# A gated unit and a long convolution on one core: an eleventh product on all rows, kernel-generation products in one block, other TensorE costs in the planner

## The chip, the cores and the metric

The kernel runs on one core of a Trainium2 chip. The metric is device time in microseconds, as the median of several runs. TensorE (PE) multiplies matrices and writes to PSUM; VectorE (DVE), ScalarE (ACT) and GpSimd (POOL) work on elements; SyncE (SP) issues most of the transfers. Each engine works through its own list of instructions in order, and waits between engines go by semaphores.

## The reference

The input is one sequence of 2048 tokens with 448 channels. The output mixes two branches with a gate per token:

```python
g = sigmoid((x * gate_w).sum(-1, keepdims=True))
# a: a long convolution per channel, its kernel a sum over 256 complex modes
dt = exp(log_dt)
A = -exp(log_A_real) + 1j * A_imag
C = (C_real + 1j * C_imag) * dt[:, None]
P = exp((A * dt[:, None])[:, :, None] * arange(2048)[None, None, :])
K = 2.0 * einsum("dn,dnl->dl", C, P).real
a = causal_convolution(x, K) + x * D_skip          # by FFT of length 4096
# b: a gated linear unit with 1792 hidden units
b = (sigmoid(x @ w_gate) * (x @ w_up)) @ w_down
out = g * a + (1 - g) * b
```

All is float32.

## The kernel before

Three streams of work share the engines.

**The gated unit** goes through the tokens in two halves H of two blocks B of 512, and through the hidden units in 14 tiles f of 128. To keep float32 accuracy with TensorE's fast format, every operand is split into a high and a low part: `wh` and `wl` of the weights, high and low blocks of the tokens in `xs`. `glu_mm` makes one 128 x 512 result in PSUM (`gu`) out of 448 input channels in eleven products. For each of three blocks of 128 channels there are three: high by high (L995), high weights by low tokens (L996), low weights by high tokens (L997). The last 64 channels are held twice, on rows 0-63 and on rows 64-127: block 3 of `xs` has the high parts of the tokens on the lower rows and their low parts on the upper rows, and block 3 of the weights holds the same 64 channels on both. So one product over 128 rows (L999) gives two of the three terms. The eleventh (L1000) takes the low weights by the high tokens, and uses rows 0-63 alone. `glu_up` calls `glu_mm` twice, for the gate and for the value, and joins them with a tanh on ScalarE (L983) and two operations on VectorE (L984, L987); `glu_down` multiplies the result by `w_down` in products of 448 columns (L1012 to L1014), and VectorE adds them up in `ob` (L1028).

**Kernel generation** (`kgen`, 28 chunks of 16 channels, each in two halves of 128 modes) computes the convolution kernels K. In a half-chunk, TensorE makes phases from positions (L827, L842), ScalarE takes sines and cosines into `ec` and `fr` (L844, L859), VectorE makes powers of the decay in `es` (three times L866) from tables `tb` that GpSimd builds, and multiplies (L881 to L885): L884 ends `ec`, L885, the last, ends `es`. Then the contraction over the modes: 16 products of 128 rows by 32 columns from `ec` and 16 from `es` (L890), all added into the one PSUM tile `kp`. `ec` and `es` have two buffers each.

**The transforms** are class `Chain`: u's spectrum, then for each half of the channels the spectrum of K, its product with u's (L500 to L507), and the way back (L546). First stages work on 64 rows (L442, L433), the spectra (L471) and the last stage (L546) on 64 columns of TensorE's array; L511 works on all of it. Two transposes go through memory by DMA (`shf`), two are done by VectorE (L453).

The order of everything is worked out when the kernel is built, by class `Plan`. Each operation is recorded with its engine, an assumed cost in ns, what it reads and writes, and a priority. `Plan.order` then runs a list schedule: at each step it takes the engine that can start first, and on it the ready operation with the smallest priority number. It follows buffers as they become free, and adds 1300 ns where ScalarE has to change its function table. The outcome is a fixed order for every engine; in the run itself only the semaphores count. Generation has priority 20, the chains of K 40 and 41, and the gated unit's products 60, so that the gated unit fills the gaps of the others. The costs of TensorE work come from `c_mm`; a group of 16 products of the generation has `KPC`, 680 ns.

Of the kernel before, what the change touches and what calls it, by code (L numbers as in the profile page):

```python
# [19 lines left out]
NCH = 28            # chunks of 16 channels  # L20
HD = 224            # channels of one half
NF = 14             # tiles of 128 hidden units
# [3 lines left out]
SPC, KPC, ACC = 640.0, 680.0, 93.0  # L26
# [17 lines left out]
# channel order of the kernel generation: (half, chunk, column tile, q)  # L44
# [8 lines left out]
def shape_tables():  # L53
    """Transform matrices and position grids: functions of the shapes alone."""
    l1, k1 = np.arange(64)[:, None], np.arange(64)[None, :]
    s1 = np.zeros((64, 32, 128), np.float32)
    t1 = np.zeros((128, 32, 64), np.float32)
    row = np.empty(64, np.int64)
    for k in range(64):
        row[k] = (k // 32) * 64 + (k % 32)  # L60
    for l2 in range(32):
        ph = 2.0 * np.pi * (((4 * k1 + 1) * (32 * l1 + l2)) % 8192) / 8192.0
        s1[:, l2, row] = np.cos(ph)
        s1[:, l2, row + 32] = -np.sin(ph)
        t1[row, l2, :] = np.cos(ph).T / 2048.0
        t1[row + 32, l2, :] = -np.sin(ph).T / 2048.0
    a, b = np.arange(32)[:, None], np.arange(32)[None, :]
    w = 2.0 * np.pi * ((a * b) % 32) / 32.0
    cw, sw = np.cos(w), np.sin(w)
    m = np.zeros((128, 256), np.float32)  # L70
    for g in range(2):
        re, im = slice(64 * g, 64 * g + 32), slice(64 * g + 32, 64 * g + 64)
        # rows (g c l2) to the real parts (g k2), then to the imaginary ones
        kr, ki = slice(32 * g, 32 * g + 32), slice(64 + 32 * g, 64 + 32 * g + 32)
        m[re, kr], m[im, kr] = cw, sw
        m[re, ki], m[im, ki] = -sw, cw
        # rows (c g k2) to rows (g c l2), the inverse
        ir, ii = slice(128 + 64 * g, 128 + 64 * g + 32), slice(128 + 64 * g + 32, 128 + 64 * g + 64)
        m[kr, ir], m[ki, ir] = cw, -sw
        m[kr, ii], m[ki, ii] = sw, cw  # L80
    pos = np.zeros((96, 16, 2, 32), np.float32)
    for d in range(16):
        pos[d, d, 0] = np.arange(32)
        pos[16 + d, d, 0] = np.arange(32)
        pos[32 + d, d, 0] = -1.0
        pos[48 + d, d, 0] = -1.0
        pos[64 + d, d, 1] = np.arange(32) + 0.5
        pos[80 + d, d, 1] = np.arange(32) + 0.5
    s1 = s1.reshape(64, 32 * 128)
    s1h = ((s1.view(np.uint32) + np.uint32(0x800)) & np.uint32(0xFFFFF000)).view(np.float32)  # L90
    return (np.concatenate([s1, s1h, s1h, s1 - s1h]), np.ascontiguousarray(t1.reshape(128, 32 * 64)),
            m, pos.reshape(96, 1024), np.eye(128, dtype=np.float32))


# functions that one table set of ScalarE holds
# [3 lines left out]
class Res:  # L99
    """Something that instructions read and write: a virtual tile or a DRAM tensor."""  # L100
# [43 lines left out]
class Plan:  # L144
    """Records instructions with what they touch, orders them for all engines by a list
    schedule (a ready instruction of the least priority number first) and emits them."""
# [9 lines left out]
    def op(self, eng, cost, fn, r=(), w=(), prio=0, after=(), size=0, table=None):  # L156
        me = dict(i=len(self.ops), eng=eng, cost=cost, fn=fn, prio=prio, size=size, table=table,
# [27 lines left out]
    def order(self):  # L185
# [14 lines left out]
        wire, table, seq, left = 0.0, (), [], len(ops)  # L200
# [15 lines left out]
        while left:  # L216
# [19 lines left out]
            if o["table"] is not None and o["table"] not in table:  # L236
                table = next(x for x in TABLES if o["table"] in x)
                cost += 1300.0
            free[e] = te + cost
# [55 lines left out]
def c_mm(n, passes=1):  # L295
    return (max(0.4167 * n, 106.0) + 3.0) * passes


# priorities, least first
# [9 lines left out]
def gated_mix(ctx: ExitStack, tc, u, ut, aim, cre, cim, ldt, dskip, gw,  # L309
# [6 lines left out]
    def dma(dst, src, size, r, w, prio, **kw):  # L316
        """dst and src: functions that give the access patterns when emitted"""
        return op("SP", SPC, lambda: nc.sync.dma_start(dst(), src()), r=r, w=w, prio=prio, size=size, **kw)
# [10 lines left out]
    us = [dt_([128, 32, HD], f"us{h}") for h in halves]       # rows (s g k2) x (r c): columns k1 = 2 r + s  # L329
# [37 lines left out]
    def evac(dst, p, w, prio, n=D):  # L367
        """dst: function that gives the access pattern"""
        op("Act", c_act(n), lambda: S.activation(dst(), p[:, :n], AF.Copy), [p], w, prio)

    class Chain:
        """a half's channels in one tile [128, 32, HD], through the stages in place"""
# [13 lines left out]
        def move(self, pool, ps, bufs):  # L386
            """later stages: other buffers, and a second place for results"""
            self.pool, self.ps, self.bufs, self.suffix = pool, (self.ps[0], ps), bufs, "x"
# [7 lines left out]
        def stage1(self, src, ap):  # L396
            """[64 l1, 32 l2, channels] -> rows (g c k1)"""
# [23 lines left out]
        def stage1_split(self, th, tl, r, l):  # L421
            """rows 0-63: high parts of the input, rows 64-127: its low parts"""
# [11 lines left out]
            op("PE", c_mm(HD, 4), f, [th, tl, y], [p], prio)  # L434
            evac(lambda: self.pair(r), p, [*xr, (x, r)], prio)

        def stage1_pair(self, tb, r, l):
# [5 lines left out]
            op("PE", c_mm(HD, 8), f, [tb, (self.x, r)], [p], self.prio)  # L443
            evac(lambda: self.pair(r), p, [(self.x, r)], self.prio)

        def transpose(self):
            """rows (g c k) x columns l become rows (g c l) x columns k"""
# [16 lines left out]
        def spectrum_pair(self, r):  # L464
            """columns k1 = 2 r + s: real and imaginary parts of rows (s g k2)"""
            p = self.psum()

            def f():
# [4 lines left out]
            op("PE", c_mm(HD, 8) + 100, f,  # L473
               [(self.x, r), *([] if self.on_dve else [(self.x, ("t", i)) for i in range(4)]), m_sb], [p], self.prio)
# [14 lines left out]
        def product(self, us):  # L489
            """the kernels' spectrum times u's, and the first stage back"""  # L490
# [6 lines left out]
        def product_pair(self, ua, r):  # L497
            x, prio, ub = self.x, self.prio, self.tile("ub", (128, 2, 2, HD))
            p = self.spectrum_pair(r)
            op("DVE", c_dve(2 * D), lambda: V.tensor_mul(      # Ur Kr, Ur Ki, Ui Kr, Ui Ki  # L500
# [10 lines left out]
            op("PE", c_mm(D, 4), lambda: T.matmul(z[:, :D], m_sb[:, 128:256], self.pair(r), start=True, stop=True),  # L511
# [3 lines left out]
        def back(self, q):  # L515
            """tiles j in [4q, 4q + 4): the first half of the tokens is stored, the others' is added to the
            gated unit's part"""
# [21 lines left out]
        def back_j(self, j, tb, o, hs):  # L539
# [3 lines left out]
            def f():  # L543
# [4 lines left out]
            op("PE", c_mm(HD, 4) + 100, f,  # L548
               [tb, (x, j), *([] if self.on_dve else [(x, ("t", i)) for i in range(4)])], [p], self.prio)
# [13 lines left out]
    def gate(q, prio):  # L563
        """tiles 4q to 4q + 3"""
# [16 lines left out]
    def params(prio):  # L581
# [22 lines left out]
        class A:  # L604
            """a tile with a view"""
# [16 lines left out]
        # dt = exp(log_dt)  # L622
# [27 lines left out]
        def frac(dst, scr):  # L650
            """dst becomes round(dst) - dst"""
            act(scr, dst, AF.Copy, bias=MAGIC)
            stt(dst, scr, MAGIC, dst, ALU.subtract, ALU.subtract)
# [9 lines left out]
        # powers r^1, r^8, r^64, r^512 of r = exp(-exp(log_A_real) dt), modes on partitions: the  # L663
        # rational form in tanh, its quotient taken by one correction of the table's exponential
# [19 lines left out]
        def silu():  # L684
            """leaves the set with sine and hyperbolic tangent"""
# [4 lines left out]
        # phase of C in turns, and 2 |C| dt  # L690
# [16 lines left out]
        tt(rt, rt, mx, ALU.add)                      # |psi| in [0, 1/2]  # L707
        ts(mx, ci, 0.0, -2.0, ALU.is_lt, ALU.mult)
        stt(mx, mx, 1.0, rt, ALU.add, ALU.mult)      # psi
# [8 lines left out]
        # frequency in turns  # L718
        per_t(ai, ai, dtp)
        w, a64 = ci, acr  # L720
        frac(ai, w)                                  # -phi
        split(ai, 4)
        act(a64, ai, AF.Copy, scale=64.0)
        frac(a64, w)                                 # 64 phi
        split(a64, 0)
        stt(mx, ai, -31.5, mx, ALU.mult, ALU.add)
        frac(mx, w)                                  # -(psi + 31.5 phi)
# [55 lines left out]
    def powers(c, bs, prio):  # L783
        """for 16 channels: r^0..7, r^(8 0..7), r^(64 0..7), amplitude r^(512 0..3)"""
# [34 lines left out]
    def turns(c, nh, i, ph, fr, tp, ec, on_pe, prio):  # L819
        """the phase x in turns, less its nearest integer"""  # L820
# [27 lines left out]
    def half_chunk(c, nh, ph, tb, kp, prio):  # L848
# [37 lines left out]
        for e in (ec, es):  # L886
            def g(e=e):
# [5 lines left out]
            op("PE", KPC, g, [e], [kp], prio)  # L893

    def kgen(c, prio):
# [20 lines left out]
        if cc == 13:  # L916
            # u D is the convolution with D at the position 0: row 0 of every column tile
# [12 lines left out]
    def glu_xz(x, z, t0, prio):  # L930
        """blocks 0-2: high parts, 4-6: low parts; block 3: high on the rows 0-63, low on the others"""
# [41 lines left out]
    def glu_up(H, f, B, pe, prio):  # L973
# [8 lines left out]
        # 2 sigmoid(g) = 1 + tanh(g / 2); the half is in og  # L982
# [7 lines left out]
    def glu_mm(x, wh, wl, cs, pe):  # L990
        p = gps.tile("gu", GUB, (128, 512))

        def g(k):
# [4 lines left out]
            else:  # L998
                T.matmul(p.real, wh[:, 3, cs], x[:, 3], start=False, stop=False)  # L999
                T.matmul(p.real, wl[0:64, 3, cs], x[0:64, 3], start=False, stop=True)  # L1000
# [103 lines left out]
def host_arrays(inputs):  # L1104
# [8 lines left out]
    w1 = np.stack([blocks(g["B_w_gate"]), blocks(g["B_w_up"])], 3)      # k p f gu c  # L1113
# [26 lines left out]
```

## Time and profile before

| what | us |
|---|---|
| median of three runs | 883.9 |
| the three runs | 888.26, 883.9, 881.62 |
| span of the profiled execution, first to last instruction | 878.0 |
| first half-chunk of generation ends on VectorE | 162 |
| last half-chunk ends | 642 |

The profile is one execution. Its own whole time isn't recorded apart from its span, so the span is set against the median: 5.9 us lie outside it. A row of the timeline, of the waits or of the groups names an engine, a line of the kernel, and the tiles it writes and reads. Matmuls are pipelined: one that starts every 0.24 us can take 0.40 us from start to end, so that PE counts as busy through short pauses, and what a product costs is read from the distance of starts. A product in full float32 leaves two records, so that a group of 16 is 32 records.

### The profile page before, as it was taken

The numbers are of one execution on the slowest core, as the hardware profiler recorded it, in microseconds if no ns is written. First come the engines' busy times: TensorE is split into PE (matmuls) and PEld (weight loads), VectorE is DVE, ScalarE is ACT, GpSimd is POOL, SyncE is SP. The second block draws the span as 40 slices with busy tenths as digits, with TensorE's granted clock in tenths as the row PEclk, the third lists the DMA queues.
The fourth block names the chain that finished last, engine by engine and source line by source line (L and its number), as shares of the span: only waits on it lengthen the run. The fifth ranks groups of instructions, "written<-read, shape, count | busy, mean of one in ns | idle before, by whom it ended". The sixth has DMA issues, their size and how long they took to land. (4 is left out here: it accounts for less than half of the span.)

```text
span 878.0 us, 16776 instructions
## 1 busy us (share of the span) xinstructions
PE 808.5 (92%) x6688; PEld 541.5 (62%) x6688; DVE 733.0 (83%) x982; ACT 501.3 (57%) x862; POOL 330.1 (38%) x358
## 2 busy tenths in 40 slices
PE   4988799999988999999998999999989999889987
PEld 2665576666655667776665666666766566445543
DVE  2869984798995999999897989899846788978995
ACT  3544654677766877777677987777722352221210
POOL 3367644454452645374355535645021120000000
PEclk9989999899997999999999999999999999998999
DMA  9951377222290326436494116422959953294324
GB/s 242 226 107 32 97 216 168 95 95 93 81 194 26 125 83 146 160 116 157 135 219 120 44 60 180 125 84 79 208 104 248 280 153 109 70 212 119 85 56 117
DMA packets 95831, 115.66 MB, mean 132 GB/s; under 512 B 31465, under 2 KB 80937, under 8 KB 95241
## 3 DMA queue, kind: packets, MB, share of 16 engines
q1 hardware_dynamic: 93704, 110.98, 48.4%
q0 software_dynamic: 2048, 3.61, 1.6%
q8 instruction: 53, 0.87, 0.4%
q14 instruction: 26, 0.20, 0.1%
HBM read 78.32 MB, written 36.24 MB: 130 GB/s over the span
## 5 line engine op out<-in xcount | busy, mean ns | idle before, releaser
L995 PE MATMUL gu_gps<-xs_glu,wh_glu 128*128 128x512 f32 x336 | 148.0, 440 | 11.7 <-ACT wh_glu L969 11.6
L866 DVE TENSOR_TENSOR es_eg<-tb_eg 128x512 f32<-128x512 f32 x168 | 125.5, 772 | 20.7 <-PE kp_egp L890 19.2
L997 PE MATMUL gu_gps<-xs_glu,wl_glu 128*128 128x512 f32 x336 | 135.3, 403 | 1.2 <-POOL wl_glu L971 1.2
L996 PE MATMUL gu_gps<-xs_glu,wh_glu 128*128 128x512 f32 x336 | 135.5, 403 | 0.0
L1012 PE MATMUL dn_gps<-vh_glu,hh_glu 128*128 128x448 f32 x224 | 98.6, 440 | 7.0 <-ACT ob_glu L1021 3.5
L971 POOL TENSOR_TENSOR wl_glu<-xr_glu,wh_glu 128x512 fp32r<-128x512 f32 x44 | 77.8, 1777 | 65.7 <-ACT wh_glu L969 65.7
L995 PEld LDWEIGHTS gu_gps<-xs_glu,wh_glu 128*128 128x128 f32 x336 | 65.6, 195 | 41.2 <-issue 19.0
L1013 PE MATMUL dn_gps<-vh_glu,hl_glu 128*128 128x448 f32 x224 | 83.7, 374 | 4.5 <-DVE hl_glu L987 4.5
L1014 PE MATMUL dn_gps<-vl_glu,hh_glu 128*128 128x448 f32 x224 | 83.6, 373 | 0.5 <-POOL vl_glu L971 0.5
L884 DVE TENSOR_TENSOR ec_eg<-ec_eg,es_eg 128x1024 f32<-128x1024 f32 x56 | 79.8, 1426 | 0.0
L997 PEld LDWEIGHTS gu_gps<-xs_glu,wl_glu 128*128 128x128 f32 x336 | 65.3, 194 | 18.0 <-POOL wl_glu L971 2.8
L813 POOL TENSOR_TENSOR tb_eg<-tb_eg 128x96 f32<-128x96 f32 (+2 forms) x84 | 73.4, 877 | 5.8
L827 PE MATMUL tp_egp<-pos_sb,ph_eg 96*128 96x512 f32 x168 | 72.5, 446 | 1.9 <-ACT fr_eg L845 1.7
L885 DVE TENSOR_TENSOR es_eg<-fr_eg,es_eg 128x1024 f32<-128x1024 f32 x56 | 73.3, 1310 | 0.3
L996 PEld LDWEIGHTS gu_gps<-xs_glu,wh_glu 128*128 128x128 f32 x336 | 65.8, 196 | 10.0 <-issue 1.3
L971 POOL TENSOR_TENSOR vl_glu<-vr_glu,vh_glu 128x448 fp32r<-128x448 f32 x24 | 35.5, 1477 | 87.0 <-ACT vh_glu L969 85.5
L1012 PEld LDWEIGHTS dn_gps<-vh_glu,hh_glu 128*128 128x128 f32 x224 | 42.9, 191 | 39.0 <-issue 17.1
L803 POOL MEMSET tb_eg<- 128x96 f32 x28 | 7.8, 283 | 152.0 <-DVE es_eg L866 152.0
L1028 DVE SCALAR_TENSOR_TENSOR ob_glu<-dn_gps,og,ob_glu 128x448 f32<-128x448 f32 x72 | 49.1, 681 | 18.4 <-PE dn_gps L1014 17.7
L859 ACT ACTIVATE ec_eg<-ec_eg,half_pi 128x1024 f32<-128x1024 f32 x56 | 63.9, 1140 | 0.0
L471 PE MATMUL fps_fups<-fx_fu,m_sb 128*64 128x224 f32 x384 | 48.7, 376 | 15.6 <-DMA fx_fu<-shf 7.8
L984 DVE SCALAR_TENSOR_TENSOR sg_glu<-sg_glu,gu_gps 128x512 f32<-128x512 f32 x56 | 38.1, 682 | 24.8 <-PE gu_gps L1000 18.1
(167 smaller groups left out, 1720.0 us busy)
## 6 DMA issues: line engine op xcount, KB each, us to landing
shf<-fx_fu SPq DMA_DIRECT2D x16, 896.0 KB
fx_fu<-shf SPq DMA_DIRECT2D x16, 896.0 KB
xr_glu<-in_w_dram SPq DMA_DIRECT2D x52, 256.0 KB
us<-fx_fu SPq DMA_DIRECT2D x4, 1792.0 KB
vr_glu<-in_w_dram SPq DMA_DIRECT2D x28, 224.0 KB
gt_pro<-in_u_dram SPq DMA_DIRECT2D x8, 448.0 KB
fx_fu<-in_u_dram SPq DMA_DIRECT2D x8, 448.0 KB
kd<-ke_eg SPq DMA_DIRECT2D x8, 448.0 KB
```

What stands on the lines that cost most here:

```text
L813: pool(96 * m, lambda n=n, m=m: G.tensor_mul(g3(n + 1, m), g3(1, m), g3(n, 1).to_broadcast([128, 32, 3, m])))
L827: T.matmul(tp.real, ph[:, c % 2, 128 * nh:128 * nh + 128].bitcast(F32R), pos[:, 512 * i:512 * i + 512], start=True, stop=last)
L866: V.tensor_mul(o.rearrange("p d (i k) -> p d i k", k=ny), x.unsqueeze(3).to_broadcast([128, 16, nx, ny]), y.unsqueeze(2).to_broadcast([128 ...
L884: op("DVE", c_dve(1024), lambda: V.tensor_mul(ec[:, :, 0:64], ec[:, :, 0:64], es[:, :, 0:64]), [es], [ec], prio)
L885: op("DVE", c_dve(1024), lambda: V.tensor_mul(es[:, :, 0:64], fr.real, es[:, :, 0:64]), [fr], [es], prio)
L971: op(eng, cost(n), lambda: e.tensor_sub(view(l), a(), view(h).bitcast(F32)), [res, (h, key)], [(l, key)], prio)
L995: T.matmul(p.real, wh[:, k, cs], x[:, k], start=(k == 0), stop=False)
L996: T.matmul(p.real, wh[:, k, cs], x[:, 4 + k], start=False, stop=False)
L997: T.matmul(p.real, wl[:, k, cs], x[:, k], start=False, stop=False)
L1012: T.matmul(p[:, :D], hh[:, ts], vh.real, start=(i == 0), stop=False)
L1013: T.matmul(p[:, :D], hl[:, ts], vh.real, start=False, stop=False)
L1014: T.matmul(p[:, :D], hh[:, ts], vl.real, start=False, stop=(i == len(fs) - 1))
```

## The change

Three things are changed.

1. The eleventh product of `glu_mm` takes all 128 rows. On the upper rows that adds the term of low weights by low tokens, which was left out before.
2. The two groups of a half-chunk, from `ec` and from `es`, become one recorded operation of 32 products, so that nothing can stand between them. It waits for both tiles.
3. The planner's costs of TensorE work are other numbers, and an operation can carry a mode: `r64` for 64 rows, `c64` and `c32` for 64 and 32 columns, none for the rest. Where the mode changes, the planner adds `SWITCH`, 145 ns.

The planned cost of a product of 512 columns goes from 216 to 227 ns, of 448 from 190 to 201, of a pair of the first stage from 872 to 759, of a pair of the spectrum from 972 to 759, of the last stage from 536 to 379, of the split first stage from 436 to 1180, and of a half-chunk's contraction from 2 x 680 to 900. Since the order comes from these costs, the order of all engines changes, with the same instructions in it. Comments are dropped as well; lines of the changed kernel stand up to 8 further down.

```diff
-SPC, KPC, ACC = 640.0, 680.0, 93.0
+SPC, KPC, ACC, SWITCH = 640.0, 900.0, 93.0, 145.0
...
+            if e == "PE" and o["mode"] != mode:
+                mode = o["mode"]
+                cost += SWITCH
             free[e] = te + cost
...
 def c_mm(n, passes=1):
-    return (max(0.4167 * n, 106.0) + 3.0) * passes
+    return max(0.4167 * n + 14.0, 195.0) * passes
+
+def c_m4(n):
+    return 2 * (0.8333 * n + 3.0)
...
-            op("PE", c_mm(HD, 4), f, [th, tl, y], [p], prio)
+            op("PE", c_mm(HD, 4) + 400, f, [th, tl, y], [p], prio, mode="r64")
...
-            op("PE", c_mm(HD, 8), f, [tb, (self.x, r)], [p], self.prio)
+            op("PE", 2 * c_m4(HD), f, [tb, (self.x, r)], [p], self.prio, mode="r64")
...
-            op("PE", c_mm(HD, 8) + 100, f,
+            op("PE", 2 * c_m4(HD), f,
...
-        for e in (ec, es):
-            def g(e=e):
+        def g():
+            for e in (ec, es):
                 for q in range(4):
                     for j in range(4):
                         T.matmul(kp[32 * j:32 * j + 32, q], e[:, 4 * j + q, 0:32], e[:, 4 * j + q, 32:96],
                                  start=nh == 0 and e is ec and q == 0,
                                  stop=nh == 1 and e is es and q == 3)
-            op("PE", KPC, g, [e], [kp], prio)
+        op("PE", KPC, g, [ec, es], [kp], prio, mode="c32")
...
                 T.matmul(p.real, wh[:, 3, cs], x[:, 3], start=False, stop=False)
-                T.matmul(p.real, wl[0:64, 3, cs], x[0:64, 3], start=False, stop=True)
+                T.matmul(p.real, wl[:, 3, cs], x[:, 3], start=False, stop=True)
```

More of the change, by code (lines that the diff above doesn't have):

```diff
@@ L154, in pool, with op @@
         return Pool(self, name, space, after, below)
-    def op(self, eng, cost, fn, r=(), w=(), prio=0, after=(), size=0, table=None):
-        me = dict(i=len(self.ops), eng=eng, cost=cost, fn=fn, prio=prio, size=size, table=table,
+    def op(self, eng, cost, fn, r=(), w=(), prio=0, after=(), size=0, table=None, mode=""):
+        me = dict(i=len(self.ops), eng=eng, cost=cost, fn=fn, prio=prio, size=size, table=table, mode=mode,
                   deps=set(), outs=[], res=[], new=[], ready=0.0, order=[a["i"] for a in after])
@@ L199, in order @@
                 cand[o["eng"]].append(o)
-        wire, table, seq, left = 0.0, (), [], len(ops)
+        wire, table, seq, left, mode = 0.0, (), [], len(ops), ""
         def start_of(o):
@@ L472, in f @@
                                  self.x[:, 2 * r + i], start=True, stop=True)
-            op("PE", c_mm(HD, 8) + 100, f,
-               [(self.x, r), *([] if self.on_dve else [(self.x, ("t", i)) for i in range(4)]), m_sb], [p], self.prio)
+            op("PE", 2 * c_m4(HD), f,
+               [(self.x, r), *([] if self.on_dve else [(self.x, ("t", i)) for i in range(4)]), m_sb], [p], self.prio, mode="c64")
             return p
@@ L510, in product_pair @@
             z = self.psum(1)
-            op("PE", c_mm(D, 4), lambda: T.matmul(z[:, :D], m_sb[:, 128:256], self.pair(r), start=True, stop=True),
+            op("PE", c_m4(D), lambda: T.matmul(z[:, :D], m_sb[:, 128:256], self.pair(r), start=True, stop=True),
                [(x, r), m_sb], [z], prio)
@@ L547, in f @@
                              start=True, stop=True)
-            op("PE", c_mm(HD, 4) + 100, f,
-               [tb, (x, j), *([] if self.on_dve else [(x, ("t", i)) for i in range(4)])], [p], self.prio)
+            op("PE", c_m4(HD), f,
+               [tb, (x, j), *([] if self.on_dve else [(x, ("t", i)) for i in range(4)])], [p], self.prio, mode="c64")
             op("DVE", c_dve(HD), lambda: V.scalar_tensor_tensor(
```

## The prediction

> **What bounds the kernel now.** I read the page's head first, then the busy time by stage, cut where the trace changes character: at 162 us, where kernel generation ends its first half-chunk (the first L885), and at 642 us, where it ends its last.
>
> ```profile
> span 878.0 us, 16776 instructions
> PE 808.5 (92%) x6688; PEld 541.5 (62%) x6688; DVE 733.0 (83%) x982; ACT 501.3 (57%) x862; POOL 330.1 (38%) x358
> ```
>
> ```profile
> 0.00:162.00 162.00, 132.92 (x479) 94.11 (x480) 117.64 (x155) 80.23 (x127) 85.96 (x65) 0.92 0.64 151
> 162.00:402.00 240.00, 231.70 (x2584) 159.58 (x2587) 217.64 (x273) 179.51 (x312) 120.59 (x145) 0.98 0.39 114
> 402.00:642.00 240.00, 230.09 (x2613) 158.15 (x2603) 217.72 (x269) 183.66 (x318) 109.45 (x129) 1.00 0.47 125
> 642.00:878.00 236.00, 213.76 (x1030) 129.67 (x1028) 180.03 (x288) 57.90 (x107) 14.08 (x21) 0.98 0.56 143
> ```
>
> A stage row gives its length, the busy time of TensorE (PE), its weight loads, VectorE (DVE), ScalarE (ACT) and GpSimd, then the granted clock, the DMA share and GB/s. In the two middle rows, kernel generation, PE is busy 461.8 of 480 us and DVE 435.4. PE bounds this stage, and DVE is right behind with 44.6 us idle. In the first stage PE is busy 82%, in the last 91%, and nothing is full.
>
> A busy PE may still waste time, so next I read its timeline by its starts (start, duration, line, operation):
>
> ```profile
> 301.17 0.40 PE L999 MATMUL gu_gps<-xs_glu,wh_glu 128*128 128x512 f32 x1
> 301.50 0.49 PE L1000 MATMUL gu_gps<-xs_glu,wl_glu 64*128 64x512 f32 x1
> 301.92 0.47 PE L1012 MATMUL dn_gps<-vh_glu,hh_glu 128*128 128x448 f32 x1
> 302.23 0.36 PE L1013 MATMUL dn_gps<-vh_glu,hl_glu 128*128 128x448 f32 x1
> 302.43 0.37 PE L1014 MATMUL dn_gps<-vl_glu,hh_glu 128*128 128x448 f32 x1
> ...
> 303.11 0.40 PE L997 MATMUL gu_gps<-xs_glu,wl_glu 128*128 128x512 f32 x1
> 303.34 0.39 PE L827 MATMUL tp_egp<-pos_sb,ph_eg 96*128 96x512 f32 x1
> ...
> 305.13 0.40 PE L996 MATMUL gu_gps<-xs_glu,wh_glu 128*128 128x512 f32 x1
> 305.37 0.40 PE L997 MATMUL gu_gps<-xs_glu,wl_glu 128*128 128x512 f32 x1
> 305.69 0.65 PE L890 MATMUL kp_egp<-ec_eg 128*32 128x64 f32 x32
> 306.28 0.98 PE L471 MATMUL fps_fups<-fx_fu,m_sb 128*64 128x224 f32 x8
> 307.19 0.65 PE L890 MATMUL kp_egp<-es_eg 128*32 128x64 f32 x32
> 307.77 0.50 PE L995 MATMUL gu_gps<-xs_glu,wh_glu 128*128 128x512 f32 x1
> 308.11 0.40 PE L996 MATMUL gu_gps<-xs_glu,wh_glu 128*128 128x512 f32 x1
> ```
>
> Between products on all 128 rows a start follows the last by 0.24 us at 512 columns (305.13 to 305.37) and 0.20 at 448 (302.23 to 302.43). Around the 64-row product L1000 it takes 0.33 (301.17 to 301.50), 0.42 and 0.31 instead. So PE pays for changing the part of its array that works, and these pauses count as busy.
>
> **First edit, L1000 on all rows.** The three starts are late by 0.09, 0.18 and 0.11 us, 0.38 in all. There are 112 such products, so up to 42.6 us of PE. In the order in which the built program lists its instructions, 17 of them stand before another product on part of the array; those keep one change and save about half: 95 x 0.38 + 17 x 0.19 = 39.3 us. The product itself keeps its 512 columns, and 303.11 to 303.34 (0.23) shows that 96 rows start like 128. The new rows hold data that is loaded already, so no DMA, ScalarE or DVE work is added. The weight loads see the same loss:
>
> ```profile
> L1000 PEld LDWEIGHTS gu_gps<-xs_glu,wl_glu x112: 182/183/286, 18.9 to 863.2; 64*128 64x128 f32 x112
> ...
>   issue: 37.6, 112
> ```
>
> That is 0.34 us of idle ahead of each load, with nothing awaited.
>
> **Second edit, the 32 products together.** Each half-chunk has an ec and an es group of 16 products (32 records). In the old order the two never stand together; 1 to 6 operations lie between. A group costs 0.08 on entry (0.32 less 0.24), 0.58 from its start to the next (307.19 to 307.77), and 0.10 more at the start after that (0.34). Two apart cost 1.52. Together, the second adds only its own run, 0.65 less one product's 0.22, so 0.43: 1.19 in all. The saving is 0.33 x 56 = 18.5 us at most; many groups have a part-array neighbour, so I take 16.
>
> **The order.** Counting changes of array part in the listed order gives 702 before and 419 after; at 0.2 each (0.38 per two), 283 fewer are 56.6 us, against 39.3 + 16 = 55.3 by the edits. By stage, up to the first group, up to the last, and after it, the counts go 62 to 5, 431 to 253, 209 to 161: 11.4, 35.6 and 9.6 us. The new costs also move gated-unit work later: 19 products of 512 columns and 3 of 448 leave the first stage, 20 of 512 leave the second, and 39 and 3 join the last. At 0.24 and 0.20 that is -5.2, -4.8 and +10.0. So PE has 16.6 us less in the first stage, 40.4 less in generation, and the same in the last.
>
> What PE is relieved of is not what the kernel gains. Who waits for PE:
>
> ```profile
> DVE es_eg L866 <- PE kp_egp L890: 19.2, 19, 3.0
> DVE ec_eg L881 <- ACT ec_eg L859: 14.9, 12, 8.3
> ...
> DVE ob_glu L1028 <- PE dn_gps L1014: 2.8, 3, 1.8
> DVE sg_glu L984 <- PE gu_gps L1000: 1.1, 3, 0.6
> ```
>
> ```profile
> ACT ec_eg L844 <- PE tp_egp L842: 39.3, 33, 2.8
> ```
>
> Both are generation alone (total us, times, longest). After the change PE needs 461.8 - 40.4 = 421.4 us there and DVE still 435: DVE is late next. The gain is that part of its 44.6 idle us which PE causes. L1028 and L984 go, 3.9. Of the 14.9 on ScalarE I take half, 7.5, because ScalarE itself waits 39.3 on PE. The 19.2 need more care. L866 overwrites an es buffer that PE must have read, and the joint group reads it later:
>
> ```profile
> 343.90 1.21 DVE L885 TENSOR_TENSOR es_eg<-fr_eg,es_eg 128x1024 f32<-128x1024 f32 x1
> 345.96 0.65 PE L890 MATMUL kp_egp<-es_eg 128*32 128x64 f32 x32
> 346.83 1.88 DVE L866 TENSOR_TENSOR es_eg<-tb_eg 128x512 f32<-128x512 f32 x3
> ```
>
> L885 ends at 345.11, PE comes to the group 0.85 us later, it ends at 346.61, and L866 follows. With ec's products ahead, the release comes 0.43 later; a freer PE comes sooner. I take half of the 19.2, 9.6. Generation gains 3.9 + 7.5 + 9.6 = 21 us; its ends are 40 (PE alone) and a loss of 24 (below). The ec group now also waits for L885, and the gated products behind it wait with it: the planner puts other work ahead, so I cost that at nothing. If that cover fails, it is up to L885's length per half-chunk, 1.21 x 56 = 68 us of PE, in a stage where PE has gained 40.
>
> In the first stage and the last DVE waits for PE as follows:
>
> ```profile
> DVE sg_glu L984 <- PE gu_gps L1000: 9.5, 3, 3.6
> ```
>
> ```profile
> DVE ob_glu L1028 <- PE dn_gps L1014: 13.7, 12, 4.4
> DVE sg_glu L984 <- PE gu_gps L1000: 7.5, 3, 3.3
> ```
>
> The first stage can gain between 0 and PE's 16.6; I take 7, three quarters of the 9.5. For the last I take 0: PE's two changes cancel. Its ends are -10 (half of the 21.2 goes) and +13, which is the 10.0 of moved products if the saved changes lie where PE was idle, with the DVE work that comes along:
>
> ```profile
> L984 DVE SCALAR_TENSOR_TENSOR sg_glu<-sg_glu,gu_gps 128x512 f32<-128x512 f32 x56 | 38.1, 682 | 24.8 <-PE gu_gps L1000 18.1
> L1028 DVE SCALAR_TENSOR_TENSOR ob_glu<-dn_gps,og,ob_glu 128x448 f32<-128x448 f32 x72 | 49.1, 681 | 18.4 <-PE dn_gps L1014 17.7
> ```
>
> Two more L984, one more L987 and one more L1028 stand there, about 3 us. SP issues the same number of transfers in another order, and GpSimd, at 38%, has room; I cost both at nothing, and they are in the +13.
>
> **Sum.** -21 - 7 + 0 = -28, so a span of 850. The median of the runs, 883.9, lies 5.9 above the profiled span; 850 + 5.9 gives **856 us**.
>
> **Rivals.**
> - *DVE and ScalarE keep their pace.* The es release eats its relief and ScalarE's waits stay: generation gains 3.9, the first stage 4: 876, between 866 and 882. For it: DVE's 435 of 480. Against: 39.3 us of ScalarE waiting on PE. Chance 0.20, half of it under 875.
> - *PE sets everything to the end.* 16.6 + 40.4 = 57 less: 827. DVE's 435 in 440 us speaks against. Chance 0.09.
> - *Slower: the es buffers.* There are two, and the first L866 of a half-chunk follows hard on the release. If PE comes to the joint group no sooner than now, each half-chunk is 0.43 longer: 56 x 0.43 = 24. With the first stage's 7 gained and the idle us kept: 878 + 24 - 7 + 5.9 = 901. It decides once PE's 0.85 us of delay does not shrink by 0.43. For it: the row at 346.83. Against: PE has 8% less to do there. Chance 0.10.
> - *Weights exposed.* Were L1000's load, 183 ns by its row, not hidden under the product before it, each would cost 0.24 + 0.18 against 0.24 + 0.38 now, and 20 us of the 39 would stay. Generation's PE need is then 421 + 58 x 0.18 = 431, still under DVE's 435; I put 4 us on it: 860. Against: 305.13 to 305.37 is a full-row product after a full-row product with no such time. Chance 0.03. [...]
> - *The change doesn't do what it says*, as the 64 rows are not what makes L1000's neighbours late. Then only the joining is left, 16 us of PE, of which a half shows: 876. Against: L890, on 32 columns, and L1000, on 64 rows, show the same signature and L827 none. Chance 0.06.
>
> **Chances and range.** The forecast has 0.52, from 842 to 868. A change under 1%, 8.8 us, can't be told from none here, the three runs themselves spreading from 881.62 to 888.26. Faster (under 875): 0.52 + 0.09 + 0.03 + half of 0.20 + half of 0.06, 0.77. Slower: the es buffers, 0.10. Same: the rest, 0.13. The range of 832 to 882 leaves out the es case, most of the PE case and little else.
>
> **What would show it.** Right: the starts around the eleventh product 0.24 apart; 56 runs of 64 records at the generation line; PE's busy share in generation down to about 92% and DVE's up to 95%; the last group's end near 614 us instead of 642; the last stage 236 us as now. Wrong: DVE's wait for the generation group well over 19 us (es buffers), or PE idle before that group until L885 (the lost cover), or a last stage over 245 us.

## The result, and the profile after

The changed kernel takes 910.7 us (908.7 to 913.9, four runs) against 882.8 before: 1.031 times as long, interval 1.026 to 1.036. The forecast was 856, between 832 and 882. It was wrong, and in sign. Here and below a time is the median of all runs, and a ratio leaves out the few runs that fell in a slower state of the chip.

The head of the page after, and the busy time by stage, cut where the first and the last half-chunk of generation end on VectorE (155 and 659 us; columns as in the prediction):

```profile
span 910.1 us, 16781 instructions
PE 794.9 (87%) x6688; PEld 562.8 (62%) x6688; DVE 734.7 (81%) x982; ACT 501.3 (55%) x862; POOL 329.2 (36%) x358
```

```profile
0.00:155.00 155.00, 115.73 (x450) 89.48 (x451) 117.25 (x154) 78.11 (x125) 79.05 (x60) 0.94 0.62 155
155.00:407.00 252.00, 230.31 (x2636) 167.11 (x2636) 221.98 (x275) 182.67 (x318) 125.99 (x154) 0.96 0.38 112
407.00:659.00 252.00, 224.41 (x2538) 164.06 (x2537) 213.09 (x263) 180.70 (x309) 109.32 (x125) 0.92 0.44 117
659.00:910.00 251.00, 224.46 (x1067) 142.19 (x1065) 182.40 (x293) 59.81 (x112) 14.81 (x21) 0.93 0.51 135
```

The 162 us of the stages before is where the first half-chunk's last operation starts; it ends at 163.4, and that of the last half-chunk at 641.5. From end to end, as in all lengths below, the first stage went from 163.4 to 154.8 us, generation from 478 to 504, and the last stage from 236.5 to 251. VectorE does the same work in generation, 435.1 us against 435.4 before, so its idle time went from 44.6 to 68.9. TensorE is busy 454.7 us there, against 461.8, but its idle time rose from 18 to 49 us, and the clock it was granted fell, from 0.98 and 1.00 to 0.96 and 0.92.

The edits themselves did what they say. TensorE's timeline after shows both (L1007 and L1008 are the old L999 and L1000, L898 the old L890):

```profile
315.45 0.40 PE L1003 MATMUL gu_gps<-xs_glu,wh_glu 128*128 128x512 f32 x1
315.69 0.39 PE L1004 MATMUL gu_gps<-xs_glu,wh_glu 128*128 128x512 f32 x1
...
316.14 0.40 PE L1007 MATMUL gu_gps<-xs_glu,wh_glu 128*128 128x512 f32 x1
316.38 0.39 PE L1008 MATMUL gu_gps<-xs_glu,wl_glu 128*128 128x512 f32 x1
316.70 0.65 PE L898 MATMUL kp_egp<-ec_eg 128*32 128x64 f32 x32
317.17 0.63 PE L898 MATMUL kp_egp<-es_eg 128*32 128x64 f32 x32
317.73 0.47 PE L1020 MATMUL dn_gps<-vh_glu,hh_glu 128*128 128x448 f32 x1
```

The eleventh product starts 0.24 us after the tenth (316.14 to 316.38), and the es group 0.47 after the ec group, in place of 0.58 and an entry. Over all 112 eleventh products the median distance is 0.23 us, where it was 0.33, and all 56 pairs of groups stand together. So what was to be saved on TensorE is there, and the loss must lie in when things run; the experiments below separate the two. TensorE's waits on shf in generation before, then TensorE's and VectorE's waits in generation after (total us, times, longest):

```profile
PE fps_fups L471 <- DMA fx_fu<-shf: 7.8, 2, 5.6
```

```profile
PE fps_fups L479 <- DMA fx_fu<-shf: 21.0, 3, 9.5
PE tp_egp L835 <- DVE fr_eg L841: 6.8, 6, 2.6
PE kp_egp L898 <- DVE es_eg L893: 5.6, 10, 1.0
PE fps_fups L450 <- DMA fx_fu<-kd: 3.5, 1, 3.5
PE fps_fups L450 <- DMA ft_fu<-in_s1t_dram: 3.1, 2, 2.7
```

```profile
DVE es_eg L874 <- PE kp_egp L898: 30.2, 15, 10.0
DVE fr_eg L841 <- ACT fr_eg L840: 11.6, 2, 7.0
DVE ec_eg L889 <- ACT ec_eg L867: 11.4, 12, 3.4
```

TensorE waited 7.8 us on shf in two waits before, and waits 21.0 in three now. The longest, 9.5 us, in the timeline of all engines:

```profile
438.12 6.79 SPq L326 DMA_DIRECT2D fx_fu<-shf  x4
...
449.08 0.39 PE L1005 MATMUL gu_gps<-xs_glu,wl_glu 128*128 128x512 f32 x1
...
449.31 0.48 SPq L326 DMA_DIRECT2D vr_glu<-in_w_dram  x1
...
452.97 0.67 DVE L992 SCALAR_TENSOR_TENSOR sg_glu<-sg_glu,gu_gps 128x512 f32<-128x512 f32 x1
458.93 1.76 PE L479 MATMUL fps_fups<-fx_fu,m_sb 128*64 128x224 f32 x8 [9.46 <-DMA fx_fu<-shf]
459.75 0.58 ACT L977 ACTIVATE vh_glu<-vr_glu 128x448 fp32r<-128x448 f32 x1 [10.03 <-DMA vr_glu<-in_w_dram]
460.40 1.13 POOL L979 TENSOR_TENSOR vl_glu<-vr_glu,vh_glu 128x448 fp32r<-128x448 f32 x1 [11.97 <-ACT vh_glu L977]
```

Four reads bring the transposed spectrum back from shf. They are issued from 438.1 on; the first product that uses them, L479, starts at 458.9. It stands at the head of TensorE's list from 449.5 on, and the generation products that VectorE needs stand behind it. VectorE has work until 453.6 and then waits too, for 10.0 us; ScalarE waits for a weight transfer that was issued behind the same reads (449.31), and GpSimd for ScalarE. The planner counts those reads at 4 x 917,504 bytes by 350 per ns, 10.5 us, and 1.5 us of latency, 12 in all. In the traces the first product that uses them starts 20.8 us after the first issue here, 21.8 and 21.9 at the other two such reads in generation, and 21.7 to 23.5 in the kernel before, each time after a wait. So a plan by these prices can put the users 9 us or more too early, in both orders.

### The profile page after: what moved, and what is told of

It reads as the page before. It is cut to its first block, busy times and chain, and to the rows that moved or that the text cites. A ratio compares the mean times of both kernels' runs of the same rounds, so it can differ in the third digit from the quotient of the medians.

```text
span 910.1 us, 16781 instructions
## 1 busy us (share of the span) xinstructions
PE 794.9 (87%) x6688; PEld 562.8 (62%) x6688; DVE 734.7 (81%) x982; ACT 501.3 (55%) x862; POOL 329.2 (36%) x358
## 5 line engine op out<-in xcount | busy, mean ns | idle before, releaser
L874 DVE TENSOR_TENSOR es_eg<-tb_eg 128x512 f32<-128x512 f32 x168 | 126.0, 773 | 37.9 <-PE kp_egp L898 30.2
L1003 PE MATMUL gu_gps<-xs_glu,wh_glu 128*128 128x512 f32 x336 | 140.7, 419 | 12.6 <-ACT wh_glu L977 10.8
L1004 PE MATMUL gu_gps<-xs_glu,wh_glu 128*128 128x512 f32 x336 | 135.9, 405 | 0.0
L1021 PE MATMUL dn_gps<-vh_glu,hl_glu 128*128 128x448 f32 x224 | 87.1, 389 | 7.4 <-DVE hl_glu L995 7.3
L835 PE MATMUL tp_egp<-pos_sb,ph_eg 96*128 96x512 f32 x168 | 76.0, 464 | 10.0 <-DVE fr_eg L841 9.1
L893 DVE TENSOR_TENSOR es_eg<-fr_eg,es_eg 128x1024 f32<-128x1024 f32 x56 | 77.9, 1390 | 0.4
L821 POOL TENSOR_TENSOR tb_eg<-tb_eg 128x192 f32<-128x192 f32 (+2 forms) x84 | 75.7, 903 | 6.0
L479 PE MATMUL fps_fups<-fx_fu,m_sb 128*64 128x224 f32 x384 | 52.0, 396 | 26.3 <-DMA fx_fu<-shf 21.0
L892 DVE TENSOR_TENSOR ec_eg<-ec_eg,es_eg 128x1024 f32<-128x1024 f32 x56 | 74.7, 1333 | 0.0
L450 PE MATMUL fps_fups<-fx_fu,ft_fu 64*128 64x224 f32 x192 | 56.1, 418 | 14.3 <-DMA ft_fu<-in_s1t_dram 5.2
L994 ACT ACTIVATE hh_glu<-sg_glu 128x512 fp32r<-128x512 f32 x56 | 35.1, 631 | 51.0 <-DVE sg_glu L992 43.0
```

The source lines that it names most:

```text
L821: pool(96 * m, lambda n=n, m=m: G.tensor_mul(g3(n + 1, m), g3(1, m), g3(n, 1).to_broadcast([128, 32, 3, m])))
L835: T.matmul(tp.real, ph[:, c % 2, 128 * nh:128 * nh + 128].bitcast(F32R), pos[:, 512 * i:512 * i + 512], start=True, stop=last)
L874: V.tensor_mul(o.rearrange("p d (i k) -> p d i k", k=ny), x.unsqueeze(3).to_broadcast([128, 16, nx, ny]), y.unsqueeze(2).to_broadcast([128 ...
L892: op("DVE", c_dve(1024), lambda: V.tensor_mul(ec[:, :, 0:64], ec[:, :, 0:64], es[:, :, 0:64]), [es], [ec], prio)
L893: op("DVE", c_dve(1024), lambda: V.tensor_mul(es[:, :, 0:64], fr.real, es[:, :, 0:64]), [fr], [es], prio)
L1003: T.matmul(p.real, wh[:, k, cs], x[:, k], start=(k == 0), stop=False)
```

## The experiments

All are compared with the kernel before on the same chip, whose median was 880 to 883 us in every group. Stage lengths and waits are from the profiled run, which for some orders lies several us under the median. Counts of products by stage are of the planned order.

**Full rows alone, in the old order.**

```diff
-                T.matmul(p.real, wl[0:64, 3, cs], x[0:64, 3], start=False, stop=True)
+                T.matmul(p.real, wl[:, 3, cs], x[:, 3], start=False, stop=True)
```

> The kernel before with the eleventh product on all 128 rows and nothing else; the order of every engine stays that of before. Theory (the new order is what costs): the row edit by itself is good, 862 to 872, because TensorE loses about 39 us of pauses and DVE can use half of it. Rival (the joined products are what costs): the same here. Rival (full rows save nothing, or load their weights in the open): 880 or more.

871.3 us, 0.986 (0.984 to 0.989). The row edit is good, at the upper end of what was expected. Generation takes 468 us in place of 478, the last stage 238, about as before.

**Full rows and joined products, old costs, so another order.** The planner gives the joint group 2 x 680 ns. Besides the row edit:

```diff
-SPC, KPC, ACC = 640.0, 680.0, 93.0
+SPC, KPC, ACC = 640.0, 1360.0, 93.0
...
+        op("PE", KPC, g, [ec, es], [kp], prio)
```

> The kernel before with full rows and the 32 products joined, all planner costs as before (1360 ns for the joined group). Theory (the new costs make the order that loses): 855 to 875. Rival (joining loses, since it holds es longer and waits for L885): 890 or more, with DVE's wait for the generation group near 30 us as in the changed kernel.

898.2 us, 1.012 (1.005 to 1.019). Neither case: worse than expected, yet VectorE's wait for the generation group is 10.7 us in generation, not 30. TensorE waits 21.2 us on shf there, as in the changed kernel, and generation takes 483 us. So an order can lose without the new costs, too.

**Full rows and new costs, the groups apart.**

```diff
-SPC, KPC, ACC, SWITCH = 640.0, 900.0, 93.0, 145.0
+SPC, KPC, ACC, SWITCH = 640.0, 450.0, 93.0, 145.0
...
-        op("PE", KPC, g, [ec, es], [kp], prio, mode="c32")
+            op("PE", KPC, g, [e], [kp], prio, mode="c32")
```

> The changed kernel with the two groups of a half-chunk recorded apart again (450 ns each, mode c32): full rows and new costs without the joining. Theory (new costs): 895 to 915, as bad as the changed kernel. Rival (joining): 870 or less.

919.4 us, 1.041 (1.036 to 1.046). The joining is not needed for the loss; the new costs lose without it. Its last stage is 277 us and holds 354 gated products of 512 columns, where the old order has 263.

**The changed kernel with 64 rows again.**

```diff
-                T.matmul(p.real, wl[:, 3, cs], x[:, 3], start=False, stop=True)
+                T.matmul(p.real, wl[0:64, 3, cs], x[0:64, 3], start=False, stop=True)
```

> The changed kernel with the eleventh product on 64 rows again; its term of low weights by low tokens is left out, as before. The order is that of the changed kernel. Theory: TensorE still sets part of the time, so the lost pauses come back in part, 918 to 935. Rival (TensorE only waits in this order): 908 to 914, no difference.

914.8 us (908.3 to 916.8) against 910.7 for the changed kernel: the rival's case, 1 us over its range. In the new order about 40 us of TensorE's pauses are worth some 4 us. Generation takes 504 us here as well.

**The joining in the old order.** The run with full rows alone, with the ec products issued together with the es products; every other instruction of every engine keeps its place.

```diff
             def g(e=e):
+                for e in (ec, es) if e is es else ():
```

> The run with full rows alone (871.3), its order of all engines unchanged, but the 16 ec products of each half-chunk held back until just before the 16 es products: the joining without a new order. Theory (the joining is harmless, the new order costs): 860 to 872, as TensorE loses some 16 us of pauses. Rival (joining itself costs through the later release of es and the wait for L885): 880 or more, with DVE's wait of L866 for L890 well over the 13 us of the run with full rows.

865.8 us, 0.979 (0.974 to 0.984). Both edits are good when nothing else moves, and this beats both kernels. VectorE's waits in generation, here and below in the same columns, show no cost of the later release of es:

```profile
DVE es_eg L866 <- PE kp_egp L891: 12.1, 12, 2.1
DVE ec_eg L881 <- ACT ec_eg L859: 12.1, 11, 6.1
```

12.1 us for the release, against 13.0 with full rows alone and 19.2 before. This run and the changed kernel have the same edits, so the new order costs 910.7 - 865.8 = 45 us. By the profiled runs, generation has 40 of it (464 to 504), the last stage 11.5 (239.4 to 250.9), and the first stage is 5 us shorter in the new order.

**The changed kernel, transfers planned slower.**

```diff
-                wire = max(wire, fin) + o["size"] / 350.0
+                wire = max(wire, fin) + o["size"] / 200.0
```

> The changed kernel, with transfers planned at 200 bytes per ns in place of 350. In the changed kernel TensorE stands 9.5 us at one reading back of shf, with the whole core idle behind it. Theory (the new order plans TensorE right but transfers too short, so TensorE meets them too early): the shf waits of TensorE fall under 8 us from 21 and the time to 880 to 897. Rival (some other property of the order): over 903.

927.7 us, 1.049 (1.045 to 1.054). A miss in the time, but a hit in its place: TensorE does not wait on shf in generation, which takes 476 us in place of 504. The last stage takes 283, with 252 products of 512 columns in it, fewer than the 302 of the changed kernel; every other transfer was planned longer too. Why the last stage is so long isn't shown.

**The changed kernel, VectorE planned slower.**

```diff
-    return 1.042 * n + 70.0
+    return 1.2 * n + 65.0
```

> The changed kernel, with VectorE planned at 1.2 n + 65 ns in place of 1.042 n + 70 (679 in place of 603 ns at 512 elements; the mean of L866 in the profile before is 772). Theory (VectorE planned too short next to a TensorE planned right, so TensorE meets its operands too early): TensorE's waits for VectorE in generation fall and the time goes to 885 to 900. Rival (order as such): over 903.

938.8 us, 1.061 (1.055 to 1.067). The theory falls for VectorE: planning it longer does not mend the order. TensorE still waits 21.1 us on shf in generation, which takes 475 us with less gated work in it; the last stage takes 300, with 404 gated products of 512 columns left for it.

**A change without meaning, in the old order.**

```diff
-    HOP, HPE = 200.0, 260.0
+    HOP, HPE = 210.0, 260.0
```

> The run with full rows alone, with the planner's hop between engines at 210 ns in place of 200: a change without meaning that makes another order. If an order is good for a reason that lies in the costs: 867 to 876. If the old order was a lucky draw (rival): 880 to 905, as the orders of the changed kernel.

877.1 us, 0.992 (0.989 to 0.995), 6 more than full rows alone and a little over what was expected. A change without meaning moves an order by several us, but this one draw not by 40.

**Less TensorE work, in the old order.** The joined run above without the product of high weights by low tokens.

```diff
-                T.matmul(p.real, wh[:, k, cs], x[:, 4 + k], start=False, stop=False)
```

> The joined run in the old order, with one of the eleven products left out: high weights by low tokens (L996 before), 336 of them, so that TensorE has 78 us less to do at 0.231 each, some 45 of them in generation. The order of everything else is unchanged. Theory (generation is set by VectorE and the waits between the engines, not by how much TensorE has to do): generation stays at 455 to 464 us and the kernel gains 15 to 30, mostly in the last stage. Rival (TensorE bounds generation, as the prediction had it): generation falls to 435 or less and the kernel gains 45 or more.

865.3 us (two runs) against 865.8. 336 products of 0.231 us, 78 us of TensorE, are gone, and the kernel is no faster. The generation row of the joined run, then of this one:

```profile
160.00:624.00 464.00, 434.37 (x5164) 320.05 (x5163) 432.59 (x539) 361.78 (x627) 228.91 (x272) 0.98 0.44 123
```

```profile
161.00:628.00 467.00, 415.65 (x4990) 294.96 (x4989) 436.03 (x538) 359.94 (x627) 221.71 (x272) 0.94 0.43 122
```

Generation stays at 464 to 467 us. 174 of the products stood there by the trace, 40 us; TensorE is busy 19 us less, and its clock fell from 0.98 to 0.94. Its idle time in generation rose from 30 to 51 us. So with both edits in, TensorE does not bound generation, though it is busy 94% of it.

**The changed kernel without the charge for a change of mode.**

```diff
-SPC, KPC, ACC, SWITCH = 640.0, 900.0, 93.0, 145.0
+SPC, KPC, ACC, SWITCH = 640.0, 900.0, 93.0, 0.0
```

> The changed kernel with the planner's charge for a change of mode at 0 in place of 145 ns. By its list 249 gated products of 512 columns stand after the last generation group, not 302 (263 before). Theory (longer planned TensorE costs push gated work out of generation, which gets no shorter for it, into the last stage): the last stage falls to 232 to 242 us from 251, the time to 870 to 895. Rival (the charge is not what costs): 903 or more.

873.9 us, 0.991 (0.987 to 0.995): 37 of the 45 us come back, in the last stage (228 us, under the expected 232 to 242) and in generation (489). This order moves gated work between the stages as well.

**The changed kernel with the old cost of a full product.**

```diff
-    return max(0.4167 * n + 14.0, 195.0) * passes
+    return (max(0.4167 * n, 106.0) + 3.0) * passes
```

> The changed kernel with the old planned cost of a full product (216 ns at 512 columns in place of 227), the charge for a change of mode kept. Its list has 247 products of 512 columns in the last stage. Theory: last stage 232 to 242 us, time 870 to 895. Rival (not these costs): 903 or more.

879.9 us, 0.997 (0.993 to 1.001). The time is as expected, the place is not: the last stage stays at 250 us with 247 products left for it, and generation falls to 469, where TensorE waits 4.4 us on shf. How many products are left does not by itself tell how long the last stage is.

**A change without meaning, in the changed kernel.**

```diff
-    HOP, HPE = 200.0, 260.0
+    HOP, HPE = 210.0, 260.0
```

> The changed kernel with the planner's hop at 210 ns in place of 200, another order without meaning; 299 products of 512 columns in the last stage. Theory (the costs decide, as they set how much work is left for the last stage): 900 to 920, as the changed kernel. Rival (the changed kernel drew a bad order by chance): below 895.

902.6 us, 1.024 (1.017 to 1.030). Another draw from the new costs is bad as well.

**Two kinds of transfer planned longer.** Only shf's reads in the chains' first part, and the first stage's matrices. The gated work of each stage stays that of the changed kernel.

```diff
-                    lambda i=i: shf.v("(gc k) l d -> gc l k d", k=32)[i], 32 * 32 * HD * 4, [shf], [(x, ("t", i))], prio)
+                    lambda i=i: shf.v("(gc k) l d -> gc l k d", k=32)[i], 32 * 32 * HD * (4 if self.suffix else 8), [shf], [(x, ("t", i))], prio)
...
-            dma(lambda: tb[0:64], lambda: s1v[0:64], 64 * TN * 512, [], [tb], self.prio)
+            dma(lambda: tb[0:64], lambda: s1v[0:64], 64 * TN * 512 * 2, [], [tb], self.prio)
```

> The changed kernel, with only two kinds of transfer planned at twice their length: the readings back of shf in the chains' first part and the first stage's matrices (ft). The gated work left for each stage stays what it is in the changed kernel (303, 627 and 302 products of 512 columns). Theory (generation lost its 26 us because TensorE meets these transfers too early and everything queued behind it stands): VectorE's idle stretches over 2 us in generation fall from 43 us to under 20, generation from 504 to 470 to 485 us, the last stage stays at 245 to 257, the time 880 to 895. Rival (the stalls only move to another wait): generation 495 or more, time over 903.

880.6 us, 1.000 (0.996 to 1.003): 30 of the 45 us come back, with the same edits and the same share of gated work by stage. Its generation and last stage (the profiled run took 874.0 us, so they flatter it by some us), then waits of TensorE and of VectorE in generation:

```profile
154.00:627.00 473.00, 444.21 (x5200) 325.35 (x5199) 443.46 (x537) 363.08 (x629) 250.25 (x277) 0.97 0.40 115
627.00:872.00 245.00, 215.92 (x1038) 137.42 (x1038) 182.14 (x292) 59.45 (x111) 13.66 (x20) 0.95 0.60 152
```

```profile
PE kp_egp L898 <- DVE es_eg L893: 7.7, 9, 1.9
PE fps_fups L450 <- DMA ft_fu<-in_s1t_dram: 6.7, 3, 3.7
```

```profile
DVE es_eg L874 <- PE kp_egp L898: 9.0, 10, 2.7
DVE ob_glu L1036 <- PE dn_gps L1022: 7.5, 4, 4.0
```

The wait on shf, 21.0 us, is gone, VectorE's for the generation group fell from 30.2 to 9.0, and generation from 504 to 473 us. Summed over the timeline, VectorE's pauses of more than 2 us in generation fell from 43 to 11. The first users of the three reads now start 25 to 31 us after the first issue, in place of 21 to 22, and none of them waits: TensorE has other work until then.

**Less TensorE work, in the changed kernel.** The same product left out as in the old order.

> The changed kernel with the product of high weights by low tokens left out, 336 of 231 ns, the order unchanged; some 19 us of it in the last stage. Theory (the last stage is 14 us longer because 39 more products stand in it): the last stage falls from 251 to 238 or less, generation stays within 8 us of 504. Rival (the last stage is set by its chain of transfers and VectorE, or by the lower clock): it stays at 246 or more.

902.4 us (two runs), 1.026 (1.018 to 1.034). The last stage takes 248 us, generation 502: the rival. The amount of TensorE work alone doesn't set the last stage, either: TensorE's idle time there rose from 27 to 35 us, and its mean clock over the profiled run fell from 0.935 to 0.895.

**No charge for modes, and the two kinds of transfer longer.**

> The run without the charge for a change of mode (873.9), with the two kinds of transfer planned at twice their length. Its list leaves 197 products of 512 columns for the last stage. Theory: generation falls from 489 to about 475, the last stage stays near 228: 855 to 868, the best of all. Rival (other waits take over, as a generation with more gated work is filled): 870 or more.

863.4 us, 0.982 (0.979 to 0.985), as good as both edits in the old order (865.8). VectorE's pauses over 2 us in generation come to 6. Generation takes 484 us with more gated work in it, the last stage 221.

## Why the prediction was wrong

*That the new order costs nothing* is the step that turned the sign. The prediction counted the gated products that change their stage, and said of the transfers only where it prices the last stage: "SP issues the same number of transfers in another order, and GpSimd, at 38%, has room; I cost both at nothing". Its sum has no term, in any stage, for a wait of TensorE on a transfer. Such waits stood in the trace before, 7.8 us on shf in generation, and the new order has 21.0 of them, with VectorE idle behind. With the same edits in the old order the kernel takes 865.8 us, in the new order 910.7: the order costs 45 us, 40 of them in generation. That is shown.

That the three reads of shf are behind most of what generation lost rests on more than one thing. Planning them and the first stage's matrices longer brings generation from 504 to 473 and the kernel from 911 to 881 us, with the same work in each stage. The time alone would not single them out: every new plan moves everything, and dropping the charge for modes or the new cost of a full product brings back as much. But TensorE's idle time right ahead of the first users of these reads, summed over the three and whatever the profile puts it down to, sorts the runs. It is 18 to 21 us in seven of them (the changed kernel, full rows and joined products in another order, full rows and new costs, 64 rows again, VectorE planned slower, the changed order without meaning, and less TensorE work in the changed kernel), and they take 898 to 939 us. It is 10 to 15 in seven others, which take 865 to 883. It is nothing in the three where these reads are planned longer; two of them take 863 and 881 us, and the third loses in the last stage. Without the charge for modes the same edit gives another 10 us (873.9 to 863.4), though there it moves gated work between the stages too.

*That TensorE bounds generation* was right in part at most. The run with 78 us less to do shows that TensorE doesn't bound it once both edits are in; for the kernel before, busy 461.8 of 480 us, that wasn't tried, but the two edits, which relieved TensorE of some 35 us in generation by the prediction's own count of the changes, shortened it by 14. The prediction took its gain from VectorE's waits and not from TensorE's relief, so its error was moderate there: in the old order both edits give 883.2 - 865.8 = 17 us where 28 were forecast. Of the 14 us by which the profiled span is shorter, generation gains 14 in place of 21, the first stage 3 in place of 7, and the last loses 3. VectorE's wait for the generation group fell by 7.1 us, where 9.6 were counted, and its wait for ScalarE by 2.8, where 7.5 were.

*The first stage*: -7 forecast, and -8.6 came out, by luck. VectorE's wait for L1000, from which the 7 were taken, is 8.5 us after and 9.5 before. With both edits in the old order the stage gained 3, so most of it came from the order, which leaves fewer gated products there.

*The last stage, 0 between -10 and +13*: it is 14 us longer, just beyond that end, and over the 245 us that the prediction named as a sign of being wrong. The 39 moved products as TensorE work don't explain it: leaving more than that out shortens the stage by 3 us. With the two transfers planned longer it is 245. What sets it stays open; the runs vary it between 221 and 300 us by the order alone.

*The rivals.* The es buffers, which gave 901, came nearest in time and were wrong in their mechanism: in the old order the joining leaves VectorE's wait for the generation group at 12.1 us, against 13.0 without it. The sign that the prediction named for them did come, 30.2 us of that wait after the change, but 10.0 of it is the stall shown above, and with the two transfers planned longer it is 9.0, with the groups joined all the same. The lost cover is real and small, 5.6 us (L898 waiting for L893). Exposed weights are refuted: L1008 starts 0.24 us after L1007. That the change doesn't do what it says is refuted by the same rows. None of the rivals had the order itself in it.

*The pauses* are about right as terms of TensorE's time: the eleventh product follows the tenth 0.09 us sooner, as counted, and a pair of groups takes 1.03 us from its start to the next product where one alone takes 0.58, so that the second adds 0.45 us, where 0.43 was counted. What they were worth to the kernel is another matter.

*What the costs do.* The new numbers are nearer to the trace for TensorE, and the order they make is worse. A possible reason: as long as TensorE was planned shorter than it is, it came later to the transfers than planned, and their short price did less harm. The runs on transfers show that their price is short; the rest is not shown. The second experiment speaks against it: with the old costs and only the groups joined, another order has the same 21 us on shf and loses as well.

## What to carry to other kernels

An engine that is busy 94% of a stage, as TensorE was in generation with both edits (434.4 of 464 us), is not thereby its bound: leave some of its work out in an unchanged order and look, before pricing what a relief is worth. Where a change alters an order that a planner makes, the order can be the larger part of the change, as here: 45 us against 17. Compare the planned length of each long transfer with the time from its issue to its first user in the trace (12 and 21 us here), and see what is queued behind that user. Planned costs that are nearer to the trace need not make a better order; test an edit in the old order first.

## What the hardware showed

TensorE given less work ran on a lower clock in both pairs of runs. Leaving 78 us out took the mean granted clock of the profiled run from 0.962 to 0.924 in the old order, and from 0.935 to 0.895 in the changed kernel. The stall shown above, in steps of 5 us:

```profile
445.00:450.00 5.00, 4.47 (x78) 3.23 (x77) 4.97 (x7) 4.34 (x9) 3.27 (x4) 1.00 1.12 212
450.00:455.00 5.00, 0.00 (x0) 0.00 (x0) 3.65 (x6) 0.00 (x0) 0.00 (x0) 0.80 1.13 205
455.00:460.00 5.00, 1.07 (x6) 0.85 (x8) 0.00 (x0) 0.25 (x1) 0.00 (x0) 0.50 0.81 213
460.00:465.00 5.00, 5.00 (x80) 2.97 (x77) 1.38 (x3) 3.96 (x8) 1.13 (x1) 0.68 0.17 51
```

TensorE's last product before the stall ends at 449.5, the next starts at 458.9. In steps of 0.1 us, where the clock changes:

```profile
452.90:453.00 0.10, 0.00 (x0) 0.00 (x0) 0.10 (x2) 0.00 (x0) 0.00 (x0) 0.94 1.00 179
453.00:453.10 0.10, 0.00 (x0) 0.00 (x0) 0.10 (x2) 0.00 (x0) 0.00 (x0) 0.50 1.21 215
...
463.10:463.20 0.10, 0.10 (x16) 0.10 (x12) 0.00 (x0) 0.10 (x1) 0.00 (x0) 0.50 0.94 359
463.20:463.30 0.10, 0.10 (x16) 0.10 (x12) 0.00 (x0) 0.10 (x1) 0.00 (x0) 0.86 0.62 233
463.30:463.40 0.10, 0.10 (x16) 0.08 (x8) 0.00 (x0) 0.10 (x1) 0.00 (x0) 1.00 0.38 143
```

The granted clock fell to 0.50 at 453.0, 3.5 us into this stall, and was back at 1.00 by 463.3, some 4.3 us after the work returned. The eight records of L479 that start at 458.93, on the lower clock, took 1.76 us; the eight that start at 463.90 took 0.98. So this stall cost more than its length.
